# Last chunk's tokens reordered at the copy into x, beta spread on TensorE, and another order of the work

## The chip, the cores and the metric

The kernel runs on one core of a Trainium2 chip. The metric is the device time of one execution in microseconds (us). Before the change it is 123.21 us, the median of three runs (123.17 to 124.2).

The engines are called PE (TensorE), DVE (VectorE), ACT (ScalarE), POOL (GpSimd) and SP (SyncE, which here only issues DMAs). Each works through its own list of instructions in order; semaphores tie them together.

## The reference

There are two stages. The first is a linear attention with product features, with B=4, H=4, S=1088, D=32 and r=8:

```
a = S1 x,  b = S2 x                  (8 numbers each per token and head)
phi(x) = outer(a, b)                 (64 numbers)
kv = sum_s phi(k)[s] v[s]^T          (64 x 32 per head)
z  = sum_s phi(k)[s]
x  = phi(q) kv / (phi(q) z + 1e-6)   (4352 tokens x 128 after joining the heads)
```

The second is a gated layer on the 4352 tokens, with d_model 128 and d_ff 2048:

```
h = x w_in;  g = h * sigmoid(beta * h);  out = g w_out
```

With beta folded into the weights, this is `out = silu(x (w_in beta)) (w_out / beta)`.

## The kernel before, in words

**The second stage.** Tokens are cut into nine chunks: eight of 512 and a last one of 256 (`LASTC`). A wave is two 128-wide slices of d_ff for one chunk (or four slices for half of chunk 0). `w1` (`W` in the order) multiplies the weights `winp` with `xT` into a PSUM tile `wave` of two banks. `silu` (`G`) has ACT read that tile and write `g` in f16. `w2` (`V`) multiplies `g` with `woutp` into `moeout`. There are 72 waves, of which the last eight have 256 tokens. `turn_out` (`O`) brings a finished chunk out to memory. Two `wave` tiles exist, so `W` can run at most two waves ahead of ACT.

Tokens lie in `xT` by (t, s): a batch's token number is 34 s + t, with s in 0..31, and `xT` holds s innermost. In chunks 0 to 7 the output is turned back by 32x32 transposes on DVE. In the last chunk `g` is the stationary operand, so the output has tokens on partitions. For its stores to be in order, `silu` writes `g` there in (s, t) order: successive f16 results go to places 8 elements apart (the branch at L396).

**The weights.** `winp` is `w_in` times beta, cut into eight pieces of 256 columns (`wi0` to `wi7`, line L293), four on POOL and four on DVE. Beta comes in three DMAs that repeat it over all 128 partitions (`beta_bc`, 1 MB in all). `woutp` (`wo0` to `wo7`) is divided by beta on ACT, DVE or POOL.

**The first stage** goes batch by batch. For batch 0 the first 512 tokens of x come by a route of their own (`s`, `q`, `gt`, `zm`, `dA`, `iA`, `nA`, `xA`): PE forms `sq`, ACT squares it to `SQ`, PE forms the denominator `den` and the numerator `numA`, DVE inverts (`iA`, L775 to L780) and multiplies (`xA`, L788) into `xT`. The keys go through `kab` (PE, copied from PSUM to SBUF), `kp` (outer products, L535, on DVE and POOL) and `kvz` (PE). The other batches use `kps`, `kp`, `kvz`, `gram`, `wz`, `qps`, `qab`, `qo`, `qt` and `nps`; `put_x` (L695) casts `nps` into `xT`.

**Order.** A string `ORDER` names every step; each engine gets its instructions in that order, and nothing is reordered later. `h`, `m` and `n` are matmuls on constants whose results nobody reads. Early in the list stand the loads; some are held back on SP by a one-column memset on POOL that must come first.

Of the kernel before, what the change touches and what calls it, by code (L numbers as in the profile page):

```python
# [20 lines left out]
def kernel(  # L21
# [37 lines left out]
    tok_chk = [(o, min(TCH, NTOK - o)) for o in range(0, NTOK, TCH)]  # L59
# [3 lines left out]
    sbA = ctx.enter_context(tc.tile_pool(name="sbA", bufs=2))  # L63
# [3 lines left out]
    start = ExitStack()  # L67
# [27 lines left out]
    beta_bc = sb([P, DFF], F32, "beta_bc")  # L95
    s12 = sb([2 * R, D], F32, "s12")
    ones = sb([P, P], F32, "ones")
    nc.vector.memset(ones, 1.0)
# [31 lines left out]
            )  # L130

    def load_win(c0, c1):
        if c0:
            nc.gpsimd.memset(w_in_sb[:, c0 : c0 + 1], 0.0)
        nc.sync.dma_start(out=w_in_sb[:, c0:c1], in_=moe_w_in[:, c0:c1])

    def load_beta(c0, c1):
        if c0:
            nc.gpsimd.memset(beta_bc[:, c0 : c0 + 1], 0.0)
        nc.sync.dma_start(  # L140
            out=beta_bc[:, c0:c1],
            in_=bass.AP(tensor=moe_beta.tensor, offset=moe_beta.offset + c0, ap=[[0, P], [1, c1 - c0]]),
        )
# [203 lines left out]
    def two(name):  # L347
        return pools()["ps2"].tile([P, 2, 512], F32, tag="two", name=name)
# [438 lines left out]
    def x_A(i):  # L787
# [57 lines left out]
    for b in range(B):  # L845
# [16 lines left out]
        Ssg y0v ok01g s0 q0 sq0 gm0 gc0c ok02v s1 gt zm lm ok00g cl kv002 ok03v kv024 lk1 zc dA0 ok04v ok05v  # L862
        ok06v lk wi1v wz0 ok07g kv046 kv068 iA0 ok08g q1 kv089 dA1 kqc iA1 lo0 lb1 nq wi2g kd0c nc nA0 xA0
        li1 wi0g lq1 tqB nA1 wc0c W xA1 G wi3g rb rv m sq2 wo0g wo1g W tk1 m qp0 G qa00 qa01 dt0v wo3g W W
        kp1 ds0 sa0v G kt1 lo1 wo2c lv1 nd0 V ny0c V G V gm1 V oq01g wi4v gc1c wi6v oK10g oq00g W wi5v t01
        oK11g G tq1 t00 wz1 W wc1c qp1 wo4v G W qa10 qa11 lk2 lq2 V wo5c G wo7v V wi7g W oK13g G dt1g nm0
        x00c x01c lv2 lk3 wo6v oK12v ds1 sa1v kv109 kd1c W G W V V oq12g oq13v oq11g W G G tk2 nd1 W ny1c O
        t13 V t11 W oq10g kp2 G G W G t10 V t12 W kt2 V nm1 G oK22v x10c x11c lq3 gm2 tq2 W G gc2v V wz2
        wc2v W G V qp2 tk3 V W G qa20 qa21 V W G lv3 dt2g V O oK23g W kp3 W V G G ds2 sa2v W V G W oq20v t20
        V V W oq22g kt3 oK21g G G V V W W G oK20g kv209 G tq3 W t22 oq21v t21 V W kd2v G G oK31v oq23v V W O  # L870
        nd2 G W G t23 V ny2v W G V nm2 gm3 x20c x21v W G V V W oK32g W G sq3 G V V W G V W G gc3v wz3 oK33g
        wc3v V O qp3 qa30 W oK30g qa31 V V dt3v G ds3 W sa3g oq32g W kv309 oq31v oq30g t31 t30 G G W V kd3c
        W V t32 G W G G V W V W G oq33g t33 V W V O G W G G nd3 ny3v V W nm3 G x30c x31v W V V V G W W G V V
        W G G V W V G O W W G G V W V W V V G G W W V V G W V G G W V W G G V W G V W V W G G V V W G V W G
        W G V W G O V O W V W V V G G W W G V V V G V V O
# [32 lines left out]
```

## Time and profile before

| | us |
|---|---|
| median of three runs | 123.21 |
| the profiled execution, its own time | 123.73 |
| its span, first to last instruction | 122.0 |
| PE busy | 100.6 |
| ACT busy | 91.0 |
| DVE busy | 62.6 |
| POOL busy | 39.6 |
| first wave of the second stage starts on PE | 18.1 |
| first ACT instruction of the last chunk starts | 99.4 |

The profile is one execution. Busy time counts instructions in flight, and a share of the whole span averages over parts with different limits, so the span is best read in three parts: up to 18.1 us (the first 512 tokens of x are made), 18.1 to 99.4 us (the eight chunks, with the attention of the other tokens in between), and 99.4 us to the end (the last chunk). The granted clock is PE's clock as the chip granted it, 1.00 being 2.4 GHz and 0.50 being 1.2 GHz.

### The profile page before, as it was taken

How to read it: one execution, taken by the hardware profiler on the slowest of the kernel's cores; microseconds unless marked ns; L12 is line 12 of the kernel's file. 1: busy time of each engine (PE TensorE's matmuls, PEld its weight loads, DVE VectorE, ACT ScalarE, POOL GpSimd, SP SyncE). 2: the span in 40 equal slices, each digit the busy share in tenths (PEclk: the TensorE clock that was granted, in tenths of full speed). 3: DMA queues.
4: the chain of work that ended last, by engine and by line, in shares of the span. 5: the costliest groups of instructions: out<-in, count | busy, mean ns of one | idle time of the engine just before them, and what ended most of it. 6: DMA issues, size and time to landing. Idle time of an engine off the chain costs nothing.

```text
span 122.0 us, 3087 instructions
## 1 busy us (share of the span) xinstructions
PE 100.6 (82%) x1260; PEld 50.4 (41%) x1261; DVE 62.6 (51%) x124; ACT 91.0 (75%) x101; POOL 39.6 (32%) x75
## 2 busy tenths in 40 slices
PE   7999868965999999999999999999899972343720
PEld 2287525631553444345454354444344431231510
DVE  3374998999999946997911475912200200200000
ACT  4014516945769886988967789977999999999960
POOL 5058906598459001893920019400000000000000
PEclk9999999999999999999999999999999999985555
DMA  3999895684578880320032050013050140050001
GB/s 106 271 247 312 292 330 231 175 185 136 235 185 222 201 220 0 52 37 5 2 57 32 0 91 1 0 29 57 8 86 0 16 70 0 3 88 0 0 0 43
DMA packets 24142, 12.27 MB, mean 101 GB/s; under 512 B 17712, under 2 KB 22080, under 8 KB 24128
## 3 DMA queue, kind: packets, MB, share of 16 engines
q1 hardware_dynamic: 23936, 12.00, 38.4%
q8 instruction: 10, 0.16, 0.6%
q10 hardware_dynamic: 192, 0.07, 0.3%
q14 instruction: 4, 0.03, 0.1%
HBM read 9.84 MB, written 2.23 MB: 99 GB/s over the span
## 4 chain that ended last, share of the span: by engine, by line
PE 50%; ACT 20%; DVE 16%; issue 10%; ACTq 0%; DVEq 0%
PE wave L376 16%; PE moeout L430 14%; ACT g L402 11%; ACT g L396 8%; PE nps L683 5%; PE h L223 4%; DVE winp L293 3%; PE kvz L547 3%; DVE kp L535 3%; PE qps L616 2%; PE kab L493 2%; DVE qt L671 1%; PE gram L561 1%; DVE o_sb L462 1%; PE kps L515 1%
## 5 line engine op out<-in xcount | busy, mean ns | idle before, releaser
L402 ACT ACTIVATE g<-wave 128x1024 f16<-128x1024 f32 x64 | 61.4, 1036 | 12.2 <-PE wave L376 11.5
L376 PE MATMUL wave<-xT,winp 128*128 128x512 f16 (+1 forms) x152 | 41.0, 361 | 11.1 <-ACT g L396 9.0
L430 PE MATMUL moeout<-g,woutp 128*128 128x512 f16 (+1 forms) x136 | 35.6, 366 | 0.4 <-DVE woutp L308 0.2
L376 PEld LDWEIGHTS <-winp 128*128 128x128 f16 x152 | 13.8, 98 | 29.3 <-issue 18.8
L430 PEld LDWEIGHTS <-woutp 128*128 128x128 f16 x136 | 12.9, 97 | 14.6 <-issue 1.1
L396 ACT ACTIVATE g<-wave 128x512 f16<-128x512 f32 x8 | 18.3, 2724 | 0.0
L462 DVE STREAM_TRANSPOSE o_sb<-moeout 128x512 f32<-128x512 f32 x8 | 5.7, 710 | 21.4 <-PE moeout L430 21.3
L535 POOL TENSOR_TENSOR kp<-kab 128x512 f32<-128x512 f32 (+2 forms) x13 | 14.6, 1131 | 3.3 <-issue 2.3
L661 POOL TENSOR_TENSOR qo<-qab 128x512 f32<-128x512 f32 (+1 forms) x9 | 12.3, 1382 | 3.6 <-DVE qab L654 3.5
L671 DVE STREAM_TRANSPOSE qt<-qo 128x512 f32<-128x512 f32 (+1 forms) x14 | 10.4, 762 | 1.5 <-POOL qo L661 1.4
L450 DVE COPY o_u<-moeout 128x128 f32<-128x128 f32 x1 | 0.3, 292 | 12.7 <-PE moeout L421 12.7
L683 PE MATMUL nps<-qt,nd 32*32 32x288 f32 (+1 forms) x256 | 6.0, 386 | 0.0
L421 PE MATMUL moeout<-woutp,g 128*128 128x128 f16 x32 | 4.1, 298 | 2.1 <-ACT g L396 2.1
L547 PE MATMUL kvz<-kp,v 128*32 128x64 f32 x288 | 5.5, 221 | 0.2 <-issue 0.2
L485 DVE STREAM_TRANSPOSE qT<-q 128x1088 f32<-128x1088 f32 (+2 forms) x5 | 5.3, 1064 | 0.6 <-DMA q<-in_q_dram 0.6
L535 DVE TENSOR_TENSOR kp<-kab 128x256 f32<-128x256 f32 (+1 forms) x8 | 5.5, 714 | 0.1
L628 DVE STREAM_TRANSPOSE qab<-qps 128x576 f32<-128x576 f32 (+1 forms) x8 | 5.2, 693 | 0.4 <-PE qps L616 0.3
L223 PE MATMUL h<-const-bfloat16-1.0 128*128 128x512 bf16 x10 | 4.6, 625 | 0.8 <-PEq L892 0.8
L547 PEld LDWEIGHTS kvz<-kp,v 128*32 128x32 f32 x288 | 4.4, 110 | 1.8 <-issue 1.4
L636 POOL TENSOR_TENSOR pac<-qab 128x288 f32<-128x288 f32 x2 | 1.7, 834 | 10.4 <-DVE qab L628 10.4
L695 ACT CAST xT<-nps 128x576 f16<-128x576 f32 (+1 forms) x6 | 3.4, 567 | 2.1 <-PE nps L683 2.0
L504 ACT COPY kab<-kab 128x192 f32<-128x192 f32 x2 | 0.5, 322 | 5.5 <-PE kab L493 5.5
(105 smaller groups left out, 96.0 us busy)
## 6 DMA issues: line engine op xcount, KB each, us to landing
v<-in_v_dram SPq DMA_DIRECT2D x12, 144.0 KB, 4.6
k<-in_k_dram SPq DMA_DIRECT2D x3, 544.0 KB, 4.1
q<-in_q_dram SPq DMA_DIRECT2D x3, 544.0 KB, 4.6
out_dram<-o_sb SPq DMA_DIRECT2D x20, 64.0 KB, 2.0
w_out_sb<-in_moe_w_out_dram SPq DMA_DIRECT2D x2, 512.0 KB, 4.8
beta_bc<-in_moe_beta_dram SPq DMA_DIRECT2D x2, 256.0 KB, 5.2
w_in_sb<-in_moe_w_in_dram SPq DMA_DIRECT2D x2, 256.0 KB, 5.7
beta_bc<-in_moe_beta_dram SPq DMA_DIRECT2D x1, 512.0 KB, 6.4
```

Source lines behind the costliest of these rows:

```text
L223: nc.tensor.matmul(out=t, lhsT=idle_w, rhs=idle_x, start=True, stop=True)
L376: nc.tensor.matmul(out=wv[:, jj // per, c : c + w], lhsT=winp[:, (j0 + jj) * P : (j0 + jj + 1) * P], rhs=xT[:, t0 + o : t0 + o + w], start ...
L396: nc.scalar.activation(out=cut(g, [[TCH, 2], [1, nt], [nt, 32]]), in_=wv[:, :, :gw].rearrange("p n (t s) -> p n t s", s=32), func=ACTF.Silu,)
L402: nc.scalar.activation(out=g[:, :, :gw], in_=wv[:, :, :gw], func=ACTF.Silu)
L430: nc.tensor.matmul(out=moe["acc"][-1][:, o : o + w], lhsT=woutp[:, j0 + jj, :], rhs=g[jj], start=head and jj == 0, stop=tail and jj == jn - 1,
L462: nc.vector.transpose(out=o_sb[:, :nt, :].rearrange("p t d -> p (t d)"), in_=moe["acc"].pop(0)[:, :tw])
L485: nc.vector.transpose(out=qT2[b % 2][:, t0:t1].rearrange("p t s -> p (t s)"), in_=q_t[b][:, t0:t1].rearrange("p t d -> p (t d)"),)
L535: eng.tensor_tensor(out=cut(KP[b][:, j0:j1], [[F, n], [R, R], [1, R]]), in0=cut(a0, [[2 * R, n], [1, R], [0, R]]), in1=cut(a0, [[2 * R, n] ...
L547: nc.tensor.matmul(out=KVZ[b][32 * h : 32 * h + 32, :F], lhsT=v_t[b][:, h, j, :], rhs=KP[b][:, j, h, :], start=(j == 0), stop=(j == NJK - ...
L661: eng.tensor_tensor(out=cut(QO[b][:, j0:j1], [[F, n], [R, R], [1, R]]), in0=cut(a0, [[32, n], [1, R], [0, R]]), in1=cut(a0, [[32, n], [0, ...
L671: nc.vector.transpose(out=QT[b][:, j0:j1].rearrange("p j h c s -> p (j h c s)"), in_=QO[b][:, j0:j1].rearrange("p j h f -> p (j h f)"),)
L683: nc.tensor.matmul(out=t[g // 2][32 * h : 32 * h + 32, g % 2, : 32 * nq], lhsT=ND[b][rows, fc, 32 * h : 32 * h + 32], rhs=QT[b][rows, :nq, ...
```

## The change

Six edits and a new order:

1. **Last chunk.** `silu` has one form for all chunks and writes `g` straight through. The (s, t) order is made earlier: a DVE copy `put_last` (`xp`) casts the last 256 tokens of batch 3 from `nps` to `xT` with the strided write. `QB[3]` becomes [0, 9, 17, 25], so that those 256 tokens lie in the last group of `nps`, and the second `put_x` of batch 3 copies one group instead of two.
2. **Beta.** The three spreading DMAs go. A DMA of 8 KB puts beta as four rows on partitions 0, 32, 64 and 96 (`beta4`), on ACT's queue. `beta_mm` (`bb0`, `bb1`) spreads it by matmuls of one row: two of 128x512 f32 each, into two banks of PSUM. The place of `bb0` comes from the pool of `wave`, that of `bb1` from `two`, which `kps`, `qps` and `nps` use too.
3. **winp.** All eight pieces are made on DVE, reading beta from PSUM.
4. **Batch 0's outer products** on DVE read one operand from the PSUM tile `kab` instead of its copy.
5. **eps.** `inv_A` adds 1e-6 by a tensor_reduce over two neighbouring elements, one of them preset, in two kept tiles `dT`.
6. **Loads.** The second quarter of `w_in` is loaded up front without a hold.

```diff
-    QB = [[16, 21, 24, 29]] + [[0, 9, 16, 25]] * 3
+    QB = [[16, 21, 24, 29]] + [[0, 9, 16, 25]] * 2 + [[0, 9, 17, 25]]
...
-    def load_beta(c0, c1):
...
-            in_=bass.AP(tensor=moe_beta.tensor, offset=moe_beta.offset + c0, ap=[[0, P], [1, c1 - c0]]),
...
+    nc.scalar.dma_start(
+        out=bass.AP(tensor=beta4.tensor, offset=beta4.offset, ap=[[32 * beta4.ap[0][0], 4], [1, DFF // 4]]),
+        in_=moe_beta.rearrange("(r c) -> r c", r=4),
+    )
...
+    def beta_mm(i):
+        t = PS["bb", i] = wave2("bb") if i == 0 else two("bb")
+        for r in range(2):
+            p = 32 * (2 * i + r)
+            nc.tensor.matmul(
+                out=t[:, r],
+                lhsT=ones[p : p + 1, :],
+                rhs=beta4[p : p + 1, :],
+                start=True,
+                stop=True,
+                tile_position=(p, 0),
+            )
-    def prep_win(i, eng):
+    def prep_win(i):
         c = slice(256 * i, 256 * i + 256)
-        eng.tensor_tensor(out=winp[:, c], in0=beta_bc[:, c], in1=w_in_sb[:, c], op=MUL)
+        b = PS["bb", i // 4].rearrange("p n c -> p (n c)")[:, 256 * (i % 4) : 256 * (i % 4) + 256]
+        nc.vector.tensor_tensor(out=winp[:, c], in0=b, in1=w_in_sb[:, c], op=MUL)
...
-        if ci == LASTC:
-            nt = gw // 32
-            nc.scalar.activation(
-                out=cut(g, [[TCH, 2], [1, nt], [nt, 32]]),
-                in_=wv[:, :, :gw].rearrange("p n (t s) -> p n t s", s=32),
-                func=ACTF.Silu,
-            )
-        else:
-            nc.scalar.activation(out=g[:, :, :gw], in_=wv[:, :, :gw], func=ACTF.Silu)
+        nc.scalar.activation(out=g[:, :, :gw], in_=wv[:, :, :gw], func=ACTF.Silu)
...
+        if b == 0 and eng is nc.vector:
+            a = PS["kab", j0 // 3 * 3][:, 64 * (j0 % 3) :]
...
+        if (b, i) == (B - 1, 1):
+            eng(out=xT[:, b * S + 32 * q0 :][:, :w], in_=PS["nps"][i][:, 0, :w])
+            return
...
+    def put_last(eng):
+        t0, tw = tok_chk[-1]
+        nt = tw // 32
+        eng(
+            out=cut(xT, [[1, nt], [nt, 32]], t0),
+            in_=PS["nps"][1][:, 1, 32 * QN[B - 1] - tw : 32 * QN[B - 1]],
+        )
...
-        nc.vector.tensor_tensor(out=rc, in0=cut(dT, [[32, 8]]), in1=eps[:, :8], op=ADD)
+        nc.vector.tensor_reduce(out=rc, in_=dT[:, :, 31:], axis=mybir.AxisListType.X, op=ADD)
...
     ORDER = """
-        h h li0 tka lb0 h mk tk00 h h h lqB h S0 Sbv Sc tk02 h Spg h h n n n tk01 j0 j1 tqA j2 sq1 y2c y1c
+        m lqB mk h h h h h tka S0 Sbv Sc h tk01 h tk00 h Spv Ssg h h lm lo0 tk02 tqA m j2 y2c j1 y1c j0 y0c
```

DVE's list just ahead of the first wave, before. `gt` feeds the denominator, `dT`, `rcA` and `rb` invert it, `xT<-numA,rb` writes x.

```order
L734 TENSOR_TENSOR gt<-gram,mk 128x256
L535 TENSOR_TENSOR kp<-kab 128x256 x4
L276 TENSOR_TENSOR lw<-lwps,mh 128x128
L293 TENSOR_TENSOR winp<-beta_bc,w_in_sb 128x256
L775 STREAM_TRANSPOSE dT<-den 128x256
L777 TENSOR_TENSOR rcA<-dT,eps 128x8
...
L788 TENSOR_TENSOR xT<-numA,rb 128x256
L485 STREAM_TRANSPOSE qT_122<-q 128x576
L788 TENSOR_TENSOR xT<-numA,rb 128x256
L302 RECIPROCAL rbeta<-bt 128x16
```

The same stretch of DVE's list with the change:

```order
L541 TENSOR_TENSOR kp<-kab_206,kab 128x256
L752 TENSOR_TENSOR gt<-gram,mk 128x256
L305 TENSOR_TENSOR winp<-bb,w_in_sb 128x256 x2
L488 STREAM_TRANSPOSE qT_125<-q 128x576
L314 RECIPROCAL rbeta<-bt 128x16
L305 TENSOR_TENSOR winp<-bb,w_in_sb 128x256 x2
L793 STREAM_TRANSPOSE dT_121<-den 128x8x32
L795 TENSOR_REDUCE rcA<-dT_121 128x8
...
L806 TENSOR_TENSOR xT<-numA,rb 128x256 x2
```

Ahead of the inversion there are now four pieces of `winp`, a transpose of q and `rbeta`; the `kp` products stand ahead of `gt` instead of behind it.

PE's list in the same stretch, before (`kvz` holds the keys' sums, `zqps` the denominator's weights):

```order
L711 MATMUL sq<-qT_122,spm 128x256 x4
L561 MATMUL gram<-kab 64x32 x9
L711 MATMUL sq<-qT_122,spm 128x256 x4
L745 MATMUL zqps<-ones,gt 64x32 x8
L273 MATMUL lwps<-s_79,sel 128x128
L547 MATMUL kvz<-kp,v 32x64 x16
L725 MATMUL den<-SQ_148,zq 32x256 x4
```

And with the change:

```order
L729 MATMUL sq<-qT_125,spm 128x256 x8
L567 MATMUL gram<-kab 64x32 x9
L293 MATMUL bb<-beta_78,ones 128x512 x2
L309 MATMUL bt<-ident,beta_jp 128x16
L763 MATMUL zqps<-ones,gt 64x32 x8
L553 MATMUL kvz<-kp,v 32x64 x36
L743 MATMUL den<-SQ_151,zq 32x256 x4
```

`gram` now stands behind both `sq`, and the spreading of beta and all of `kvz` stand ahead of the denominator. The second `numA` (not shown), which stood behind the first `xT` product, now stands ahead of it.

ACT's list at the end, before:

```order
L695 CAST xT<-nps 128x576
L402 ACTIVATE g<-wave 128x1024 x17
L396 ACTIVATE g<-wave 128x2x8x32 x8
L450 COPY o_u<-moeout 128x128
```

And with the change:

```order
L704 CAST xT<-nps 128x576
L702 CAST xT<-nps 128x288
L405 ACTIVATE g<-wave 128x1024 x17
L405 ACTIVATE g<-wave 128x2x256 x8
L453 COPY o_u<-moeout 128x128
```

The last eight activations lose the form of four-level writes, and a smaller cast stands ahead.

## Rows read from the trace of the kernel before

**Rows 1.** The page's head.

```profile
span 122.0 us, 3087 instructions
```

**Rows 2.** Groups: line, engine, tiles, count | busy us, mean ns | idle before.

```profile
L402 ACT ACTIVATE g<-wave 128x1024 f16<-128x1024 f32 x64 | 61.4, 1036 | 12.2 <-PE wave L376 11.5
L396 ACT ACTIVATE g<-wave 128x512 f16<-128x512 f32 x8 | 18.3, 2724 | 0.0
```

**Rows 3.** Chain that ended last, from the last chunk on: start, us, what.

```profile
88.76 0.43 PE moeout L430 x2
...
118.42 0.30 DVE o_u L450
```

**Rows 4.** Stretches: us, busy by engine (count), granted clock, DMA share, GB/s.

```profile
15.00:20.00 5.00, 3.80 (x51) 1.72 (x56) 4.50 (x12) 1.98 (x6) 0.90 (x4) 1.00 0.95 338
...
105.00:110.00 5.00, 1.90 (x16) 1.60 (x16) 0.72 (x1) 5.00 (x3) 0.00 (x0) 0.87 0.34 56
...
18.15:30.50 12.35, 9.28 (x148) 5.35 (x149) 11.80 (x19) 7.72 (x14) 9.55 (x14) 1.00 0.63 183
...
18.15:99.40 81.25, 77.02 (x1006) 36.55 (x1008) 50.29 (x79) 67.03 (x80) 30.71 (x37) 1.00 0.36 87
```

**Rows 5.** Timeline of ACT: start, us, instruction and count [idle before].

```profile
43.09 1.31 ACT L695 CAST xT<-nps 128x576 f16<-128x576 f32 x2 [0.78 <-PE nps L683]
...
91.98 7.44 ACT L402 ACTIVATE g<-wave 128x1024 f16<-128x1024 f32 x8 [0.20 <-PE wave L376]
...
99.41 18.31 ACT L396 ACTIVATE g<-wave 128x512 f16<-128x512 f32 x8
```

**Rows 6.** Timeline of PE in the last chunk.

```profile
98.93 0.38 PE L376 MATMUL wave<-xT,winp 128*128 128x256 f16 x2
...
99.15 0.59 PE L430 MATMUL moeout<-g,woutp 128*128 128x512 f16 x2
...
106.65 0.38 PE L421 MATMUL moeout<-woutp,g 128*128 128x128 f16 x4
...
113.61 1.48 PE L421 MATMUL moeout<-woutp,g 128*128 128x128 f16 x12
```

**Rows 7.** Chain of waits at the start.

```profile
6.73 1.95 PE kab L493 x18
8.68 1.10 PE sq L711 x8
...
17.03 0.43 DVE xT L788
...
18.15 0.56 PE wave L376 x4
```

**Rows 8.** Timeline of DVE up to 27 us.

```profile
10.94 0.42 DVE L734 TENSOR_TENSOR gt<-gram,mk 128x256 f32<-128x256 f32 x1 [2.03 <-ACT gs L573]
11.28 2.31 DVE L535 TENSOR_TENSOR kp<-kab 128x256 f32<-128x256 f32 x4
...
13.71 0.75 DVE L293 TENSOR_TENSOR winp<-beta_bc,w_in_sb 128x256 f16<-128x256 f32 x1
14.38 0.44 DVE L775 STREAM_TRANSPOSE dT<-den 128x256 f32<-128x256 f32 x1
...
17.37 0.77 DVE L485 STREAM_TRANSPOSE qT<-q 128x576 f32<-128x576 f32 x1
...
23.42 3.60 DVE L293 TENSOR_TENSOR winp<-beta_bc,w_in_sb 128x256 f16<-128x256 f32 x3
```

**Rows 9.** Timeline of PE: its two longest idle times from 18 to 30 us.

```profile
27.07 0.60 PE L376 MATMUL wave<-xT,winp 128*128 128x512 f16 x2 [1.14 <-DVE winp L293]
28.98 0.78 PE L616 MATMUL qps<-qT,qw 32*32 32x288 f32 x32 [1.30 <-DVE qT L485]
```

**Rows 10.** Timeline of POOL, its first piece of winp.

```profile
12.32 0.99 POOL L293 TENSOR_TENSOR winp<-beta_bc,w_in_sb 128x256 f16<-128x256 f32 x1 [0.49 <-DMA beta_bc<-in_moe_beta_dram]
```

**Rows 11.** DMA issues: queue, count, KB each, median us to landing.

```profile
out_dram<-o_sb SPq DMA_DIRECT2D x20, 64.0 KB, 2.0
```

More of the change, by code (lines that the diff above doesn't have):

```diff
@@ L94 @@
     w_out_sb = sb([P, NJ, P], F32, "w_out_sb")
-    beta_bc = sb([P, DFF], F32, "beta_bc")
+    beta4 = sb([P, DFF // 4], F32, "beta4")
     s12 = sb([2 * R, D], F32, "s12")
@@ L132, in load_win @@
     def load_win(c0, c1):
-        if c0:
+        if c0 >= DFF // 2:
             nc.gpsimd.memset(w_in_sb[:, c0 : c0 + 1], 0.0)
         nc.sync.dma_start(out=w_in_sb[:, c0:c1], in_=moe_w_in[:, c0:c1])
-    def load_beta(c0, c1):
[L138 to L141, printed above, removed]
-            in_=bass.AP(tensor=moe_beta.tensor, offset=moe_beta.offset + c0, ap=[[0, P], [1, c1 - c0]]),
-        )
     def load_wout(j0, j1):
@@ L160 @@
     load_v(0)
-    load_beta(0, DFF // 4)
     load_win(0, DFF // 4)
+    load_win(DFF // 4, DFF // 2)
     ident = sb([P, P], F32, "ident")
@@ L178 @@
     nc.vector.memset(pmv[64:], -0.25)
-    eps = sb([P, NJK], F32, "eps")
-    nc.vector.memset(eps, 1e-6)
+    dTs = [sb([P, 8, 33], F32, f"dT{i}") for i in range(2)]
+    for t in dTs:
+        nc.vector.memset(t[:, :, 32:], 1e-6)
     qT2 = [sb([P, T, 32], F32, f"qT{n}") for n in range(2)]
@@ L533, in outer_k @@
         a0 = KAB[b][:, j0:j1]
+        a = a0
         n = H * (j1 - j0)
+        if b == 0 and eng is nc.vector:
+            a = PS["kab", j0 // 3 * 3][:, 64 * (j0 % 3) :]
         eng.tensor_tensor(
             out=cut(KP[b][:, j0:j1], [[F, n], [R, R], [1, R]]),
-            in0=cut(a0, [[2 * R, n], [1, R], [0, R]]),
+            in0=cut(a, [[2 * R, n], [1, R], [0, R]]),
             in1=cut(a0, [[2 * R, n], [0, R], [1, R]], R),
@@ L773, in inv_A @@
     def inv_A(i):
-        dT = sbA.tile([P, 8, 32], F32, tag="dT", name="dT")
-        nc.vector.transpose(out=dT.rearrange("p t c -> p (t c)"), in_=PS["den"][:, HA * i : HA * i + HA])
+        dT = dTs[i]
+        nc.vector.transpose(out=dT[:, :, :32], in_=PS["den"][:, HA * i : HA * i + HA])
         rc = RC["A"] = sbA.tile([P, 8], F32, tag="rcA", name="rcA")
-        nc.vector.tensor_tensor(out=rc, in0=cut(dT, [[32, 8]]), in1=eps[:, :8], op=ADD)
+        nc.vector.tensor_reduce(out=rc, in_=dT[:, :, 31:], axis=mybir.AxisListType.X, op=ADD)
         nc.vector.reciprocal(out=rc, in_=rc)
@@ L794 @@
     DO = {
-        "h": lambda: keep_warm("h", 1), "m": lambda: keep_warm("m", 3), "n": lambda: keep_warm("n", 1),
+        "h": lambda: keep_warm("h", 1), "m": lambda: keep_warm("m", 3), "n": lambda: keep_warm("n", 1), "bb0": lambda: beta_mm(0), "bb1": lambda: beta_mm(1),
         "lqB": lambda: load_rows(q, q_t, 0, "q", ((NA, T),)),
         "lo0": lambda: load_wout(0, NJ // 2), "lo1": lambda: load_wout(NJ // 2, NJ),
-        "li0": lambda: load_win(DFF // 4, DFF // 2), "lb0": lambda: load_beta(DFF // 4, DFF // 2),
-        "lb1": lambda: load_beta(DFF // 2, DFF),
         "li1": lambda: load_win(DFF // 2, DFF),
@@ L806 @@
         "rb": prep_rbeta, "rv": rbeta_dve,
+        "xp": lambda: put_last(VC),
         "W": w1, "G": silu, "V": w2, "O": turn_out,
@@ L818 @@
         for i in range(8):
-            DO[f"wi{i}{e}"] = lambda i=i, eng=eng: prep_win(i, eng)
             DO[f"wo{i}{e}"] = lambda i=i, eng=eng: prep_wout(2 * i, 2 * i + 2, eng)
@@ L835 @@
     for i in range(8):
+        DO[f"wi{i}"] = lambda i=i: prep_win(i)
         DO[f"wo{i}c"] = lambda i=i: wout_act(2 * i, 2 * i + 2)
@@ L860 @@
     ORDER = """
-        h h li0 tka lb0 h mk tk00 h h h lqB h S0 Sbv Sc tk02 h Spg h h n n n tk01 j0 j1 tqA j2 sq1 y2c y1c
[L862 to L875, printed above, removed]
+        m lqB mk h h h h h tka S0 Sbv Sc h tk01 h tk00 h Spv Ssg h h lm lo0 tk02 tqA m j2 y2c j1 y1c j0 y0c
@@ new lines @@
+        ok02v s1 q1 lk ok04v ok07g ok08g s0 ok00v ok03v ok01v cl gm0 gt lk1 ok05g gc0c bb0 wi1 wi3 rb zm
+        kv002 kv024 q0 tqB ok06g kv046 kv068 kv089 rv sq1 zc dA0 kqc wz0 wc0c wi2 wi0 sq0 nq nc dA1 wo3c n
+        kd0c iA0 lo1 n iA1 n nA0 nA1 wo0g li1 xA0 W lq1 G xA1 tk1 qp0 qa00 qa01 dt0v ds0 nd0 ny0c W W wo2v
+        lv1 kp1 kt1 wo1c V sa0g G wo5c oq01g tq1 W wo4c V G bb1 wi4 gm1 lk2 gc1v V W lq2 G G wi5 W G wi6
+        oq00g oK10g wi7 t01 wz1 wc1v lv2 oK11g t00 V qp1 qa10 qa11 tk2 W V oK12g dt1v ds1 W V wo6c lk3 G G
@@ new lines @@
+        nm0 oK13g kv109 x00c x01c W W G G wo7v sa1v oq11v t11 V oq12v t12 V O W kp2 W kd1c nd1 G G kt2 W V G
+        ny1v W oq10g G oq13g V t10 t13 W oK23g tk3 oK22v gm2 lq3 G nm1 x10v gc2c wz2 W V V V x11v oK20g W
+        wc2c G G oK21v lv3 W V V V tq2 W G G O sq2 qp2 qa20 qa21 dt2v V V ds2 W W G kv209 W kd2v sa2g oq23v
+        G oq22g V W kp3 G W V G G kt3 W V oq20g W G t22 t23 V W nd2 G W G V W G G V oK33g t20 ny2v W G gm3
+        oq21g t21 gc3v nm2 x20c tq3 x21c wz3 wc3c O W oK31v sq3 V V W G V V W G G V W V G W G V V W G O qp3
@@ L876 @@
+        qa30 V qa31 dt3v ds3 sa3g W G V oK32v W G V W V G W G V W V oq32v G W G oq30v V V W G W oK30v oq33v
+        O G t33 oq31g kv309 kd3c W G t30 W G t31 nd3 V t32 W G ny3v nm3 xp W V V x30c x31c V G W G W V V W G
+        G V W V W G G O W V G W V W G G V W G V W V W V G G W V W V O G G W G V W V W V G V W V G G W G W V
+        G W G V W V W V G W V V G G W G V V V O V V O
     """
```

1 line of the change is left out of this document (removed).

## The prediction, as it was made before the changed kernel ran

> **What bounds the kernel now.** I read the page's head first: the span is 122.0 us [rows 1]. The profiled execution took 123.73 us, so 1.73 us lie around the span; its time stands 0.5 us above the median of 123.21. Next I read the costliest groups [rows 2]. Look at the two silu groups together: 64 activations of 1024 elements and 8 of 512, and the smaller ones are the longer. The timeline of ACT [rows 5] gives the spacing that counts: eight full ones in 7.44 us, 0.93 us each, but eight half ones in 18.31 us, 2.29 us each. ACT is busy without a break from 99.41 us to the last products. So the last chunk is bound by ACT, and by a price that half the work should not have.
>
> Third come the stretches [rows 4]. From 18.15 to 99.40 us PE is busy 77.02 of 81.25 us: this part is bound by PE. Of the 4.2 us that it is idle there, 3.1 lie between 18.15 and 30.50 us (busy 9.28 of 12.35). Two waits make most of them: 1.14 us for DVE's `winp` and 1.30 us for DVE's transpose of q [rows 9]. From 105 us on the granted clock falls (0.87 over 105 to 110 us), after PE had little to do.
>
> Last I read the chain at the start [rows 7]: `kab`, `sq`, and through DVE to `xT` at 17.03 us, then PE's first wave at 18.15 us. DVE's own timeline [rows 8] shows what stands in a row there.
>
> So there are three parts in series: a start bound by a chain, a middle bound by PE, and a tail bound by ACT. A saving in any of them moves the end.
>
> **The tail.** PE reaches the last chunk's first wave at 98.93 us [rows 6], and the output copy starts at 118.42 [rows 3], just after the last product. I call this 19.5 us. What will it be?
>
> - ACT's side. A straight write of 512 elements is not in this trace. The bounds are half a full activation, 0.465 us, and a cast of 576 elements, 0.655 us (two in 1.31 [rows 5]). I take 0.56, between the two, as 512 is near 576 but the fixed part must be in it. At 98.93 us ACT still has 0.48 us to go to its first half activation (99.41). Then 0.48 + 8 x 0.56 + the last four products at 0.38 [rows 6] = 5.3 us.
> - PE's side. Eight pairs of 256-column matmuls take 0.22 each (99.15 - 98.93 [rows 6]), 1.76 in all. In the changed order four pairs of 512-column products of the chunk before still stand behind the first of them, one more than before, 4 x 0.43 [rows 3] = 1.72. The 32 products of 128 columns took 0.38 for four at the full clock [rows 6], 0.095 each, 3.04 in all. The sum is 6.5 us.
>
> PE's side is the longer, so I take 6.5 us; the ends are 5.3 (ACT's side alone) and 7.9 (the products at half clock, 1.48/12 = 0.123 us each [rows 6], and half a us of waiting for each other). This term is 6.5 - 19.5 = **-13.0 us**.
>
> The strided write does not vanish: `put_last` does it on DVE, 256 elements. At the rate of ACT's old write (2.29 us for 512) that would be 1.15 us, at least 0.38 (as half of the 576-element transpose in [rows 8]). It stands some sixteen waves ahead of its reader, where DVE has little to do, so I cost it at nothing. If that cover were gone it would be 1.15 us. The shortened cast on ACT is under that same cover.
>
> A rule bears on this. The row shows 2.29 us for half the elements at a step of 16 bytes. The Trainium skill, "SBUF — State Buffer", section "Door 1: The DMA port swizzle", says both that each access to a new 16-byte line pays and that a stride of up to 8 two-byte elements is free; the second sentence, read literally, clears exactly this step. By it the price would have another source, and the tail would keep its 19.5 us. That is rival three.
>
> **The middle.** Three things change. First, one pair of products moves into the tail: -0.4 us. Second, `bb1` is new on PE. This trace has no matmul of one row; the nearest is `sq`, f32, which takes 1.10 us for 2048 record columns (8 records of 256 [rows 7]). `bb1` has the same number if each of its two matmuls is two records of 512. I take +1.1 us, with half of it and twice as ends (0.55 and 2.2), since rows of 1 may overlap more or less than rows of 64. Third, the waits of [rows 9]: four pieces of `winp` are done before the first wave, and the last four come from PSUM behind the q transpose for the next batch. The pieces that held PE took 1.2 us each (three in 3.60 us [rows 8]) while POOL was working; `gt`, which has the same size and also reads PSUM, took 0.42. The fifth wave still has to wait for the transpose and for `wi4`, but waves six to eight follow at once. Of the 3.1 idle us I take back 2.0; the ends are 0 and 3.1. The sum of the middle is -0.4 + 1.1 - 2.0 = **-1.3 us**. The two constant matmuls and the small turn of beta that leave this part I leave out of the sum: less than half a microsecond.
>
> **The start.** Here the change adds to a chain. On PE, `gram` now waits behind both `sq` blocks, one more of 1.10 us, and `kab` starts some 0.4 us later behind `lwps` and one more constant matmul. So `gt` starts at about 12.0 instead of 10.94 us (where it waited for ACT's copy), and the `kp` products that stood behind it, 2.31 us [rows 8], are now done while it waits. Then `bb0` takes 1.1 us on PE, and the first `winp` can start at 13.1. On DVE follow four pieces of `winp` at 0.45 = 1.8, the transpose of q 0.65 (0.77 with its overlap), `rbeta` 0.2, the inversion 17.03 - 14.38 = 2.65, and `xT` 0.43 [rows 8, 7]: 18.8. The first wave used to wait a second `numA` behind `xT` (17.46 to 18.15); now it does not, so it starts at 18.85, against 18.15. I take **+0.7 us**. PE's own chain to the denominator (`zqps`, `kvz`, `den` behind `bb0`) is done before DVE asks for it by this count. The ends: -0.5 if `gt` comes as early as now, +3.7 if the four `winp` cost 1.2 each. PE's clock I leave at 1.00, as in the stretch from 15 to 20 us with 3.80 of 5 us busy [rows 4].
>
> The megabyte of beta that is no longer loaded I cost at nothing: the one wait for it is 0.49 us on POOL [rows 10], off the chain.
>
> **The end.** Chunk 7's four stores are issued on SP while the last eight waves run, and now these take 6.5 instead of 19.5 us. The final stores can land behind them; one such store takes 2.0 us [rows 11]. I add **+0.3 us** (0 to 1.0). From 118.42 on everything else stays.
>
> **The sum**: 123.73 - 13.0 - 1.3 + 0.7 + 0.3 = 110.4 us for an execution like the profiled one, and 0.5 less for the median: **110 us**.
>
> **The rivals.**
>
> 1. *DVE becomes the bound of the start.* All eight `winp` are on it now. For it: the three pieces at 1.2 us each. Against: they read two operands from SBUF, while `gt` reads one from PSUM at 0.42. With +3.7 instead of +0.7 and no idle time won back, 110 + 3 + 2 = 115; with the first alone, 113. Chance 0.13.
> 2. *The start costs nothing and the idle time goes.* -0.7 and -1.1 from the middle, and the tail on ACT's side, -1.2: 107. For it: PE has a queue of products to fill the waits. Chance 0.12.
> 3. *The change does not do what it says*: the half activations keep 2.29 us although they write straight. For it: no row here shows a straight one of 512. Against: the casts, which are straight and larger, take 0.655. (It is the case that the Trainium skill's "SBUF — State Buffer", read literally, would have.) Without the -13.0 and with the rest at -0.3 the time is 123. Chance 0.03.
> 4. *PE loses its full clock* (slower). The place is the start and what follows it: if DVE keeps PE waiting long enough there, the granted clock goes to 0.5, and the PE-bound middle runs at half speed until it is back. Each us of PE work at half clock costs one more, so it decides from 13 us of such work; 19 us of it give 129. Against: 1.00 in 15 to 20 us at 3.80 of 5 busy; the clock fell only when PE was busy 1.90 of 5 us. Chance 0.02.
>
> My forecast keeps 0.70. The range 107 to 113.5 holds it with its bounds, rival 2, and the nearer half of rival 1. Less than one per cent can hardly be told from no change here. Faster by over 1%: forecast and the first two rivals, 0.95. Within 1%: rival 3, 0.03. Slower: rival 4, 0.02.
>
> **What would show it.** In the profile after: the last eight silu spaced by 0.5 to 0.7 us, and PE without long gaps in the tail at a clock of 1.00; `winp` at about 0.45 us a piece, all on DVE; `bb` at 1.1 us twice; the first wave near 18.9 us; less than 1.5 us of PE idle in the 12 us after it. It would be wrong if the spacing stays above 1 us, if PE idles beyond 2 us between the first wave and the tail, or if the first wave comes after 21 us.

## The result, and the profile after

The changed kernel takes 108.01 us (107.54 to 108.68) against 123.25 us before. Here and below, times are medians over executions, and they, the ratios and the intervals leave out executions that took over 1.5% more than the fastest of the same kernel, such as one of 116.63 us here (with it the median is 108.34). The ratio is 0.8753, with a 95% interval of 0.8675 to 0.8832. The prediction was 110 us, in a range of 107 to 113.5. The profiled execution took 108.68 us; its span is 106.9 us, so 1.78 us lie around it, as 1.73 did before.

These are the page's head and the one silu group that is left; it answers to both groups of [rows 2].

```profile
span 106.9 us, 3093 instructions
L405 ACT ACTIVATE g<-wave 128x1024 f16<-128x1024 f32 (+1 forms) x72 | 65.5, 992 | 9.7 <-PE wave L388 9.2
```

In ACT's timeline, three half activations of the last chunk take 1.88 us:

```profile
98.86 1.88 ACT L405 ACTIVATE g<-wave 128x512 f16<-128x512 f32 x3
```

Next the stretches, to be read against [rows 4]: the 12.4 us around the first wave, the whole middle, and the tail. The columns are those of before.

```profile
18.60:31.00 12.40, 11.46 (x189) 6.27 (x189) 11.54 (x24) 9.86 (x17) 8.10 (x12) 1.00 0.78 231
...
18.60:97.00 78.40, 75.95 (x1001) 36.10 (x1001) 50.19 (x84) 66.29 (x84) 23.65 (x28) 1.00 0.34 81
97.00:104.00 7.00, 5.89 (x58) 4.24 (x56) 1.01 (x2) 5.54 (x10) 0.00 (x0) 1.00 0.36 58
```

In the first line PE is idle 0.94 us, of which 0.63 lie ahead of the first wave; before it was 3.1. The clock is 1.00 in all three.

The tail in PE's timeline, to be read against [rows 6], and then the output copy on DVE:

```profile
97.24 0.38 PE L388 MATMUL wave<-xT,winp 128*128 128x256 f16 x2
...
100.53 0.39 PE L424 MATMUL moeout<-woutp,g 128*128 128x128 f16 x4
...
101.01 0.61 PE L424 MATMUL moeout<-woutp,g 128*128 128x128 f16 x8
...
101.67 1.31 PE L424 MATMUL moeout<-woutp,g 128*128 128x128 f16 x20
103.02 0.29 DVE L453 COPY o_u<-moeout 128x128 f32<-128x128 f32 x1 [1.79 <-PE moeout L424]
```

From the last chunk's first wave to the copy it is 5.78 us (103.02 - 97.24); before, 19.49. In the chain of waits PE has this stretch from 98.37 us on:

```profile
98.37 0.38 PE wave L388 x2
...
101.83 1.16 PE moeout L424 x20
```

ACT's timeline shows what bounds the part ahead of it. These lines are ACT's two casts of batch 3, and its last 21 activations:

```profile
80.05 0.64 ACT L704 CAST xT<-nps 128x576 f16<-128x576 f32 x1 [0.95 <-PE nps L689]
81.50 0.40 ACT L702 CAST xT<-nps 128x288 f16<-128x288 f32 x1 [0.81 <-DVE xT L713]
...
85.72 16.81 ACT L405 ACTIVATE g<-wave 128x1024 f16<-128x1024 f32 x21
```

ACT has no idle time in the last 16.8 us ahead of the copies. PE waits a little for each wave there: the middle ends bound by ACT, not by PE, as it already did before for its last 7.44 us [rows 5].

The start in the chain of waits, to be read against [rows 7]:

```profile
7.15 2.19 PE kab L496 x18
9.34 2.03 PE sq L729 x16
11.37 0.70 PE gram L567 x18
12.07 1.06 PE bb L293 x4
...
13.73 1.14 PE kvz L553 x72
14.87 0.42 PE den L743 x7
...
15.61 0.61 PE den L743 x8
...
18.87 0.32 DVE xT L806
...
19.23 0.61 PE wave L388 x4
```

And DVE's timeline there, to be read against [rows 8], with the later pieces of `winp` last:

```profile
13.18 0.76 DVE L305 TENSOR_TENSOR winp<-bb,w_in_sb 128x256 f16<-128x256 f32 x2 [0.64 <-PE bt L309]
...
16.24 0.45 DVE L793 STREAM_TRANSPOSE dT<-den 128x256 f32<-128x256 f32 x1 [0.87 <-PE den L743]
...
25.93 1.08 DVE L305 TENSOR_TENSOR winp<-bb,w_in_sb 128x256 f16<-128x256 f32 x3
```

Three pieces of `winp` take 1.08 us where three took 3.60. The transpose `dT` waits 0.87 us for the *second* `den`, although it reads the first.

| term (us) | predicted | measured | from |
|---|---|---|---|
| tail | -13.0 | -13.7 | 19.49 to 5.78 |
| middle | -1.3 | -2.8 | 98.93 - 18.15 = 80.78 to 97.24 - 19.23 = 78.01 |
| start | +0.7 | +1.1 | 18.15 to 19.23 |
| end | +0.3 | +0.3 | 122.0 - 118.42 = 3.58 to 106.9 - 103.02 = 3.88 |
| sum | -13.3 | -15.1 | 123.73 to 108.68 |

### The profile page after: what moved, and what is told of

Same layout as the page of the kernel before. It is cut to its first block, busy times and chain, and to the rows that moved or that the text cites. A ratio compares the mean times of both kernels' runs of the same rounds, so it can differ in the third digit from the quotient of the medians.

```text
span 106.9 us, 3093 instructions
## 1 busy us (share of the span) xinstructions
PE 97.9 (92%) x1268; PEld 50.0 (47%) x1269; DVE 61.7 (58%) x132; ACT 78.4 (73%) x108; POOL 30.2 (28%) x62
## 4 chain that ended last, share of the span: by engine, by line
PE 52%; ACT 22%; DVE 14%; DMA 4%; issue 2%; POOL 1%; SPq 1%; DVEq 0%; ACTq 0%
ACT g L405 21%; PE wave L388 16%; PE moeout L433 13%; PE nps L689 5%; DMA k<-in_k_dram 4%; PE kvz L553 3%; PE gram L567 3%; DVE qt L677 2%; DVE qo L667 2%; PE kab L496 2%; PE bb L293 2%; PE sq L729 2%; PE moeout L424 2%; PE qps L622 1%; DVE qab L634 1%
## 5 line engine op out<-in xcount | busy, mean ns | idle before, releaser
L405 ACT ACTIVATE g<-wave 128x1024 f16<-128x1024 f32 (+1 forms) x72 | 65.5, 992 | 9.7 <-PE wave L388 9.2
L388 PE MATMUL wave<-xT,winp 128*128 128x512 f16 (+1 forms) x152 | 40.1, 356 | 2.5 <-DVE xT L806 1.2
L667 POOL TENSOR_TENSOR qo<-qab 128x512 f32<-128x512 f32 (+1 forms) x8 | 11.6, 1454 | 2.6 <-DVE qab L660 2.4
L541 POOL TENSOR_TENSOR kp<-kab 128x256 f32<-128x256 f32 (+2 forms) x11 | 11.2, 1027 | 1.6 <-DVE kab L529 0.9
L660 POOL TENSOR_TENSOR qab<-qab,rc 128x288 f32<-128x288 f32 (+1 forms) x3 | 2.2, 730 | 29.3 <-DVE rc L655 29.3
L667 DVE TENSOR_TENSOR qo<-qab 128x512 f32<-128x512 f32 (+1 forms) x6 | 5.5, 929 | 0.8 <-POOL qab L660 0.8
L553 PE MATMUL kvz<-kp,v 128*32 128x64 f32 x288 | 4.8, 220 | 0.0
L689 PEld LDWEIGHTS nps<-qt,nd 32*32 32x32 f32 x256 | 3.2, 103 | 2.4 <-DVE nd L614 1.0
L482 DVE STREAM_TRANSPOSE kTs<-k 128x1088 f32<-128x1088 f32 x3 | 3.8, 1276 | 0.0
L567 PEld LDWEIGHTS gram<-kab 128*64 128x64 f32 x72 | 2.6, 137 | 1.9 <-issue 1.9
```

What stands on the lines that cost most here:

```text
L388: nc.tensor.matmul(out=wv[:, jj // per, c : c + w], lhsT=winp[:, (j0 + jj) * P : (j0 + jj + 1) * P], rhs=xT[:, t0 + o : t0 + o + w], start ...
L541: eng.tensor_tensor(out=cut(KP[b][:, j0:j1], [[F, n], [R, R], [1, R]]), in0=cut(a, [[2 * R, n], [1, R], [0, R]]), in1=cut(a0, [[2 * R, n], ...
L553: nc.tensor.matmul(out=KVZ[b][32 * h : 32 * h + 32, :F], lhsT=v_t[b][:, h, j, :], rhs=KP[b][:, j, h, :], start=(j == 0), stop=(j == NJK - ...
L567: nc.tensor.matmul(out=t[c : c + 64, : H * R], lhsT=KAB[b][:, j].rearrange("p h c -> p (h c)"), rhs=KAB[b][:, j, :, :R], start=(j < 2), st ...
L667: eng.tensor_tensor(out=cut(QO[b][:, j0:j1], [[F, n], [R, R], [1, R]]), in0=cut(a0, [[32, n], [1, R], [0, R]]), in1=cut(a0, [[32, n], [0, ...
L689: nc.tensor.matmul(out=t[g // 2][32 * h : 32 * h + 32, g % 2, : 32 * nq], lhsT=ND[b][rows, fc, 32 * h : 32 * h + 32], rhs=QT[b][rows, :nq, ...
```

## The experiments

**1. What in the old silu cost 2.29 us?** The last chunk's eight activations of the kernel before, each written another way.

```diff
+            ap = ([[1, gw]], [[32, 8], [1, 32]], [[1, 2], [2, 128]], [[1, 4], [4, 64]],
+                  [[1, 8], [8, 32]], [[1, 16], [16, 16]], None, [[1, 8], [8, 32]])[kind]
+            # None: straight write, in_=cut(wv, [[512, 2], [1, 32], [32, nt]])
-                out=cut(g, [[TCH, 2], [1, nt], [nt, 32]]),
+                out=cut(g, [[TCH, 2]] + ap),
```

> The kernel before, with the last chunk's eight silu activations (2x256 elements each) written in eight different ways: straight; straight in pieces of 32; at steps of 2, 4, 8 and 16 f16 elements (4, 8, 16 and 32 bytes); straight with the permuted reading of PSUM instead (steps of 32 f32); and at a step of 8 again. The output's tokens of the last chunk are therefore not in order. Theory (the step of the write is the price): straight and in pieces of 32 about 0.5 to 0.6 us spacing, step 8 2.29 us as in the kernel before, step 16 at least that; steps 2 and 4 in between or cheap. Rival A (the number of levels of the pattern is the price): pieces of 32 as dear as step 8, 2.3 us. Rival B (the limit lies above 16 bytes, as the Trainium skill's 'SBUF - State Buffer' reads literally): step 8 is not dear for its step, only 16 would be. Rival C (a permuted read is as dear as a permuted write): the reading form 2.3 us too. Total by the theory: some 123.2 less five to six times 1.7, about 113.

It took 115.45 us (one execution; 2.4 us above the expected total, which counted five or six cheap activations where four are cheap). The chain of waits runs through ACT, so the starts of its pieces are the spacing:

```profile
98.80 0.58 ACT g L406
...
99.43 0.43 ACT g L406
...
99.92 0.59 ACT g L406
...
100.55 0.60 ACT g L406
...
101.60 0.74 ACT g L406
...
103.63 2.64 ACT g L406
```

And the permuted read in ACT's timeline:

```profile
105.80 0.89 ACT L399 ACTIVATE g<-wave 128x512 f16<-128x512 f32 x1
```

One activation of each kind is read here. Straight takes 0.63 us to the next start, pieces of 32 take 0.49, a step of 2 elements 0.63, of 4 1.05, of 8 2.03, of 16 2.17. So it is the step of the write, not the levels of the pattern: rival A falls. Rival B falls too. The step of 8 is dear, and the step of 4 (8 bytes) is not free. The permuted read lasts 0.89 us where a straight activation of that size lasts about 0.6: rival C falls, the read costs far less than the write. The Trainium skill, "SBUF — State Buffer", section "Door 1: The DMA port swizzle", says that each access to a new 16-byte line pays, and the 2.03 us at a step of 16 bytes agree; its allowance of 8 two-byte elements does not hold here, and the measurement decides.

**2. The last chunk's edit alone, on the kernel before.**

```diff
-        if ci == LASTC:
-            ...
+        nc.scalar.activation(out=g[:, :, :gw], in_=wv[:, :, :gw], func=ACTF.Silu)
-        ... x30c x31v W ...
+        ... x30c x31v xp W ...
```

(with `QB[3]`, `put_x` and `put_last` as in the change.)

> The kernel before with the last chunk's edit alone: straight silu writes, the strided write made once by DVE's put_last behind the second put_x. Theory (the tail is most of the gain): the last chunk goes from 19.5 to 5.8 us on its stretch as in the changed kernel, so 123.25 - 13.7 = 109.6 us, 109 to 110.5. Rival (start and middle bring a large part, and a faster tail only exposes another wait): 113 or more.

It took 111.68 us, ratio 0.9063 (0.9001 to 0.9126), so 11.7 us less than before: over three quarters of the whole gain, but 2 us later than the theory. The tail itself is as expected: 99.26 us (first wave) to 104.88 (copy), 5.6 us in the trace. Two things are new elsewhere. The first is `put_last` (L699), in DVE's timeline and then in PE's:

```profile
82.55 1.28 DVE L699 CAST xT<-nps 128x256 f16<-128x256 f32 x1
```

```profile
83.98 1.02 PE L376 MATMUL wave<-xT,winp 128*128 128x512 f16 x4 [0.65 <-DVE xT L699]
```

The second tile of `nps` lies in one of the two places of the `wave` pool, and PE's next wave waits 0.65 us until `put_last` has read it. From the start of batch 3's `nps` to the last chunk's first wave it is 19.36 us (99.26 - 79.90) against 18.55 before (98.93 - 80.38): 0.8 of the 2 us. The second is the clock. The stretches of this kernel at 26 to 32 us:

```profile
26.00:28.00 2.00, 0.70 (x15) 0.24 (x24) 2.00 (x3) 1.36 (x3) 2.00 (x5) 1.00 0.07 16
28.00:30.00 2.00, 2.00 (x36) 0.57 (x36) 2.00 (x4) 0.51 (x2) 1.09 (x1) 0.67 0.91 309
30.00:32.00 2.00, 2.00 (x6) 0.47 (x4) 2.00 (x5) 0.76 (x1) 1.13 (x2) 0.50 0.61 245
```

After the waits of [rows 9] (PE busy 0.70 of 2 us) the granted clock falls to 0.50, that is 1.2 GHz, for about 3 us. In the profiled execution of the kernel before it stayed at 1.00 after the same waits. Whether the fall costs time is the question of experiment 6.

**3. The last chunk's edit alone taken back from the changed kernel** (the reverse of that diff).

> The changed kernel with the last chunk's edit alone taken back (strided silu writes, no put_last, both groups by put_x). Theory: 108.3 + 13.7 = 122 us, less up to 0.8 since ACT no longer waits for put_last: 121 to 122. Rival (the new order has the last chunk's work placed so that the dear writes overlap more): below 119.

It took 121.24 us, ratio 0.9839 (0.9799 to 0.9879), as the theory had it. ACT's timeline has the old spacing again, 2.29 us each:

```profile
96.23 18.32 ACT L408 ACTIVATE g<-wave 128x512 f16<-128x512 f32 x8
```

So the tail is worth 13.2 us with the new order (121.24 to 108.01), and the rest of the change 2.2 us without the new tail (123.4 to 121.24) and 3.7 with it (111.68 to 108.01).

**4. The second half of beta by DMA instead of PE.** `winp` stays on DVE in its place, but reads both operands from SBUF.

```diff
-        b = PS["bb", i // 4]...
+        b = beta_hi[:, 256 * (i - 4) : 256 * (i - 4) + 256] if i >= 4 else PS["bb", i // 4]...
-        ... G bb1 wi4 gm1 ...
+        ... G wi4 gm1 ...          (lbh, the 512 KB load, ahead of iA1)
```

> The changed kernel with the second half of beta spread by DMA (512 KB into SBUF) instead of by the second bb on PE; winp pieces 4 to 7 stay on DVE at their places but read both operands from SBUF. Theory (the place of the operand sets the price of winp while POOL works): pieces 4 to 7 take 0.7 to 1.2 us instead of 0.36, PE waits for them between 25 and 30 us, 1.3 to 3.4 us longer there, less 1.06 us of bb: 108.5 to 110.5 us. Rival (the order alone took the waits away): pieces 0.4 to 0.5 us, and the 1.06 us of PE are saved: about 107.3 us.

Only one execution counts, the profiled one, at 109.95 us, so the finding rests on its trace. DVE's timeline, and PE's:

```profile
24.03 1.41 DVE L313 TENSOR_TENSOR winp<-beta_hi,w_in_sb 128x256 f16<-128x256 f32 x1
...
25.47 2.72 DVE L313 TENSOR_TENSOR winp<-beta_hi,w_in_sb 128x256 f16<-128x256 f32 x3
```

```profile
25.50 0.60 PE L396 MATMUL wave<-xT,winp 128*128 128x512 f16 x2 [0.75 <-DVE winp L313]
26.71 0.61 PE L396 MATMUL wave<-xT,winp 128*128 128x512 f16 x2 [0.60 <-DVE winp L313]
```

The pieces take 1.41 and 0.91 us instead of 0.36, and PE waits for them, 1.35 us in these two lines. The rival falls: it is the operand in PSUM that makes `winp` cheap here, where POOL works beside it, not only the order. What POOL's part in it is, no run shows. The saving is more than the 1.06 us of PE that `bb1` costs: without `bb1` it is 13.06 us from the first wave to the first `nps` (31.61 - 18.55), and 11.38 in the changed kernel (30.61 - 19.23), though not all of that lies in these two waits.

**5. put_last the other way round, and iA0 ahead of dA1.** Both come from the profile after: ACT's cast waits 0.81 us for `put_last`, and `dT` 0.87 us for the second `den`. The changed kernel ran beside them.

> The changed kernel unaltered, on the same chip as the three beside it, for comparison: 107.5 to 108.7 us.

It took 108.17 us, ratio 0.8761 (0.8724 to 0.8798). First the reading form:

```diff
-            out=cut(xT, [[1, nt], [nt, 32]], t0),
-            in_=PS["nps"][1][:, 1, 32 * QN[B - 1] - tw : 32 * QN[B - 1]],
+            out=xT[:, t0 : t0 + tw],
+            in_=cut(PS["nps"][1], [[1, 32], [32, nt]], 512 + 32 * QN[B - 1] - tw),
```

> The changed kernel with put_last turned round: it reads PSUM at steps of 32 f32 and writes x straight. Theory (the strided write of 1.30 us is on the path: ACT's second cast of batch 3 waits 0.8 us for it, and from there to the end ACT has no idle time): DVE's put_last 0.3 to 0.5 us, the cast follows the one before it at once, total 0.8 us less, about 107.5 us. Rival A (a permuted read of PSUM costs as much as a permuted write): put_last 1.3 us again, no change. Rival B (put_last is covered, as the prediction had it): put_last shorter, total unchanged within 0.2 us.

It took 107.72 us, ratio 0.8733 (0.8690 to 0.8775). In the changed kernel `put_last` takes 1.30 us on DVE. Here it takes 0.42, and ACT's cast no longer waits. From DVE's and ACT's timelines:

```profile
79.93 0.42 DVE L713 CAST xT<-nps 128x256 f16<-128x256 f32 x1 [1.72 <-PE nps L689]
```

```profile
79.87 0.64 ACT L704 CAST xT<-nps 128x576 f16<-128x576 f32 x1 [0.94 <-PE nps L689]
80.54 0.40 ACT L702 CAST xT<-nps 128x288 f16<-128x288 f32 x1
```

So rival A falls in the trace. From that first cast to the first wave of the last chunk it is 16.6 us (96.45 - 79.87) against 17.2 beside it (96.84 - 79.64): 0.6 us less, so rival B falls there as well. In the time of the whole kernel the difference, 0.4 us, is not resolved, since the intervals overlap.

Then the order:

```diff
-        sq0 nq nc dA1 wo3c n kd0c iA0 lo1 n iA1 ...
+        sq0 nq iA0 nc dA1 wo3c n kd0c lo1 n iA1 ...
```

> The changed kernel with the first inversion (iA0) ahead of the second denominator (dA1) in the order; nothing else moved. Theory (DVE waited 0.87 us for the second den although it needs the first, and the start goes one to one to the end): dT starts at 15.4 instead of 16.2 us, the first wave at 18.4 instead of 19.2, total 0.8 us less, about 107.5 us. Rival A (den then waits for the transpose, so the second inversion comes as late as now): first wave at 19.0 or later, total unchanged. Rival B (the start is given back later, since ACT bounds the last 16 us): first wave earlier, total unchanged.

It took 108.36 us, ratio 0.8816 (0.8773 to 0.8858): no gain. `dT` starts at 14.88 us instead of 15.83, but of this 0.95 us only 0.37 reach the first wave (18.45 against 18.82). DVE then waits 0.47 us for `numA`, which stands on PE behind the constant matmuls:

```profile
17.97 0.76 DVE L806 TENSOR_TENSOR xT<-numA,rb 128x256 f16<-128x256 f32 x2 [0.47 <-PE numA L743]
```

This is near rival A, with another next in line than the one I named. Whether 0.37 us goes on to the end was too little to measure.

Both edits together:

> Both edits together (put_last reading at steps, iA0 ahead of dA1). Theory: the gains add, since one is in the start and the other in the last third: 1.6 us less, about 106.7 us. Rival: whichever of the two is given back, 107.5 us or more.

107.44 us, ratio 0.8716 (0.8676 to 0.8756), and a second time, on another chip:

> The changed kernel with put_last reading at steps and iA0 ahead of dA1, again, for comparison with the run beside it: 107.0 to 107.7 us.

107.34 us, ratio 0.8709 (0.8670 to 0.8747). Both medians lie below the changed kernel's 108.17, by 0.7 and 0.8 us, with intervals that overlap. It is the fastest kernel here, and that it beats the changed one is likely, not shown. The expected 106.7 us was not reached.

Last, that kernel without the constant matmuls ahead of `numA`. The expectation speaks of two of the three; the edit takes out all three:

```diff
-        ... dA1 wo3c n kd0c lo1 n iA1 n nA0 ...
+        ... dA1 wo3c kd0c lo1 iA1 nA0 ...
```

> a_best_again without the last two of the three constant matmuls ahead of numA (0.8 us on PE, on which numA and so the first xT product wait 0.47 us). Theory: the first wave starts 0.3 to 0.47 us earlier and the end too, 106.7 to 107.2 us. Rival (they keep the clock up): granted clock below 1.00 after 17 us, and a time of 107.5 us or more.

Inconclusive: the two executions that count took 107.67 and 108.94 us (ratio 0.8803, 0.8743 to 0.8862). They show no gain, and settle neither the theory nor its rival.

**6. Does the fall of the clock cost time?** The kernel of experiment 2 again, and beside it the same with constant matmuls in PE's idle time.

```diff
-        oK11g G tq1 t00 wz1 W wc1c qp1 ...
+        oK11g G tq1 t00 z5 wz1 W wc1c z6 qp1 ...    (z5, z6: five and six matmuls 128x512)
```

> The kernel before with the last chunk's edit alone, again, for comparison on the same chip as b_warm: 111 to 112.6 us, mean granted clock 0.975 to 0.98, with the clock at 0.5 for some 3 us from about 28.5 us on, after PE was busy 1.6 of 4 us from 24 to 28 us.

> b_tail2 with eleven matmuls on constants (128x512 bf16, results unread) put into the two idle times of PE from 24 to 28 us, five ahead of wz and six ahead of qps; nothing else moved. Theory (the idle time costs twice: once as waiting, and again since the granted clock falls after it): the clock stays at 1.00 there, mean near 1.00, and 1.5 to 2 us are saved, 109.5 to 110.5 us. Rival A (the clock falls for another reason): mean 0.975 again, 111 to 113 us. Rival B (the half clock was hidden by DVE, which bounds that stretch): clock 1.00, time unchanged within 0.4 us.

110.84 us (109.58 to 111.10; ratio 0.8989, 0.8941 to 0.9036) without, 109.82 (109.61 to 110.42; 0.8934, 0.8898 to 0.8970) with them. The two stretches, first without:

```profile
24.00:28.00 4.00, 1.56 (x42) 0.39 (x34) 4.00 (x5) 2.63 (x5) 4.00 (x6) 0.94 0.45 110
28.00:32.00 4.00, 4.00 (x70) 1.56 (x65) 4.00 (x7) 1.54 (x2) 1.64 (x5) 0.64 0.59 237
```

and with them:

```profile
24.00:28.00 4.00, 3.03 (x21) 1.27 (x21) 4.00 (x5) 1.59 (x3) 4.00 (x6) 1.00 0.87 191
28.00:32.00 4.00, 4.00 (x91) 1.60 (x96) 4.00 (x7) 2.72 (x5) 1.64 (x2) 1.00 0.76 274
```

With them the clock stays at 1.00 in the profiled execution. That does not settle rival A, since three of the four executions without them had a mean clock of 0.998 or more as well. The fifth wave to the first `nps` takes 7.2 us with them (24.11 to 31.34) and 8.0 without (23.31 to 31.32), but little of that is left further on: from the first wave to batch 3's `nps` it is 62.70 us with them (79.60 - 16.90) and 62.84 without (79.08 - 16.24). And the three executions without the fall took 110.8 to 111.1 us, longer than the one with it (109.58). So the fall is not what sets the time of that kernel, and the theory's 1.5 to 2 us are not there. This is nearest to rival B; that it is DVE that hides the half clock is not shown. The medians differ by 1.0 us, with intervals that overlap, and what that is stays open. What does show in both traces is `put_last`: from batch 3's `nps` to the last chunk's first wave they take 19.37 and 19.36 us, the 0.8 us of experiment 2 again.

## Why the prediction was right, point by point

- **What bounds it.** Right. Taking back the last chunk's edit alone gives 121.24 us, and doing it alone 111.68. The dear thing was the step of the write, as experiment 1 shows by itself; rival 3 is refuted by it. The last 7.44 us of the middle were ACT's already, without a break [rows 5].
- **The tail.** The mechanism and the side were right: ACT's half activations come 0.6 us apart, and PE sets the end. The term was 0.7 us too small a gain, because the products of 128 columns were priced at 0.095 us, from a row of four. Such a row has about 0.15 us besides its products: four take 0.39 us, eight 0.61 and twenty 1.31. The chain after has 20 of them in 1.16 us, 0.058 each: 32 x 0.037 = 1.2 us, of which some went to waiting.
- **put_last costs nothing.** This step failed. DVE had the time, as I said, but ACT's cast of the same PSUM tile was made to wait for it (0.81 us), and ACT has no idle time from there on. I looked at the reader of `xT`, sixteen waves later, and not at who else uses the source. The trace points to the source, not the target: the cast before it reads the other tile of `nps`, writes `xT` too, and runs beside `put_last` (starts at 80.05 and 80.11 us). In experiment 2 the one held up is PE, by 0.65 us, since the source is also a place for a wave. The price, 1.30 us, lay above my upper end of 1.15. Turning it round gives back 0.6 us in the trace.
- **The middle.** The mechanism was right, its size was off. `bb` took 1.06 us, as estimated from `sq`. The waits taken back were 2.8 us, not 2.0 (PE idle 0.3 us after the first wave instead of 3.1), and the pieces of `winp` took 0.36 us and not 0.45. Experiment 4 shows that the operand in PSUM is the reason for the cheap pieces; that they make up the whole 0.8 us is not shown. The remaining 0.7 us lie in PE's work. From the first wave to the last chunk it is 76.55 us before and 76.19 after, where the sum has 0.7 more: 1.1 us too much. The two constant matmuls and the small turn of beta that I left out are some 0.6 of it (0.22 each and 0.17, by starts in the trace of experiment 2), the other 0.5 stay open. PE idle time after 31 us went the other way, from 1.16 us (4.23 - 3.07) to 1.51 (2.45 - 0.94).
- **The start.** The count on PE and DVE was right up to `winp` (`gt` at 12.11 against 12.0 predicted, `bb` done at 13.13 against 13.1). One sentence failed: PE's own chain was not done before DVE asked. `dT` waited 0.87 us for the second `den`, because the order has both ahead of the first inversion. The cheaper `winp` gave 0.35 us of that back (0.76 + 0.69 for four pieces instead of 1.8), so the term was off by only 0.4 us: the two errors have opposite signs, which is luck.
- **The end.** Right, and 0.2 of the 0.3 us for the reason given. SP issues chunk 7's four stores from 101.26 to 103.44 us, so its last store goes out at 103.54, 0.52 us behind the start of the copy. Before, those four were out by 107.70 us and it was 0.32 (118.74 - 118.42). In experiment 2 it is 1.22 (106.10 - 104.88).
- **The range.** Its ends are not the sum of the terms' ends, which together give 105.6 to 118.1 us. The terms were off by -0.7 (tail), -1.5 (middle) and +0.4 us (start), and the total by -1.7.
- **Rivals.** Rival 1 did not come: all eight `winp` on DVE are cheap (0.36 to 0.42 us each). The changed kernel went part of the way to rival 2 (the idle time goes, and the tail is short), without its free start. Rival 4 has its mechanism seen in experiment 2, at the place that I named, but in a kernel with the old start, and there the fall left 0.1 us in the traces (experiment 6), not one us for each us of PE's work; in the changed kernel the clock is 1.00 throughout.

## What to carry to other kernels

Where an activation with half the elements takes longer than one with all, look at the step of its output: the permutation is cheaper as a strided read of PSUM, done once, than as a strided write done eight times. Price a moved step by everything that touches its source and its target, not by its reader alone. Ask also whose place the source takes while it waits to be read. Price short matmuls from a long row of them, as each row in the tail, short or long, has the same 0.15 us on top.

## What the runs showed of the hardware that was not expected

- ACT, f16 output, 512 elements, start to start, one activation of each kind: 0.49 to 0.63 us straight or at a step of 4 bytes, 1.05 at 8 bytes, 2.03 at 16, 2.17 at 32. It grows from 8 bytes on and hardly beyond 16.
- DVE pays too: 256 f16 elements at a step of 16 bytes take 1.30 us, and 0.42 written straight with a read of PSUM at steps of 128 bytes.
- DVE's f32 product of 256 elements takes 0.36 to 0.42 us with one operand in PSUM, and 0.9 to 1.4 us with both in SBUF, at the same place in the program with POOL busy beside it.
- A f32 matmul of one row and 512 columns takes 0.53 us here (two in 1.06), as much as the same columns of 64 rows in `sq`.
- The same kernel kept the full clock in some executions and not in others: the kernel of experiment 2 had a mean granted clock of 0.975 to 0.978 in five executions and of 0.998 or more in three, with PE busy 1.56 of 4 us ahead of the fall in the one that was profiled in experiment 6.
